# A second Strassen level in the first feed-forward product, with its weight forms streamed from DRAM

## The chip, the core and the metric

The kernel runs on one core of one Trainium2 chip. The metric is the device time of one execution in microseconds, the median of several runs. Work is done by TensorE (matrix products, into the eight PSUM banks of 512 fp32 columns), VectorE, ScalarE and GpSimd (elementwise work), and SyncE, which here only issues DMA transfers. Each engine takes its own instructions in program order and waits for others through semaphores.

## What is computed

Attention over 8 batches, 12 heads, 448 positions and 64 dimensions, with q and k normalized, and then a feed-forward net on the 3584 x 768 result. All in fp32; the two weight matrices come as float64 and are converted by the kernel during unit 0 ("words" in the code).

```python
q_n, k_n = rmsnorm(q, g_q), rmsnorm(k, g_k)
attn = softmax(q_n @ k_n.T / sqrt(64))          # per batch and head
x = (attn @ v).transpose(0, 2, 1, 3).reshape(8 * 448, 12 * 64)
h = np.maximum(x @ w_in, 0.0)                   # w_in 768 x 2048
out = h * h @ w_out                             # w_out 2048 x 768
```

## The kernel before, in words

**Units.** Two batches make a unit (896 rows of x); there are four units, 0 to 3. The feed-forward net of unit u runs while attention makes the x of unit u+1. Attention goes over pairs of heads, 12 pairs per unit; the result of a pair is one tile xT of 128 partitions (two heads' dimensions) by 448 columns (positions), kept transposed. Attention of the first unit runs alone; the last unit's feed-forward net runs alone.

**First level of Strassen.** Both feed-forward products use the Winograd form of Strassen's scheme: seven half-size products P1 to P7 take the place of eight, with sums of the operands ("forms") made before and sums of the products after. For the first product the x of a unit is cut into a 2 x 2 of blocks (by batch, and by the half of the 768 features), and w_in likewise (by halves of features and of hidden columns). `make_x_forms` (L640) and `begin_forms` (L651) turn three chunks each of the x blocks 11, 12, 21, 22 into the seven right-hand operands 11, T1, 21, T2, 22, T3, T4, by two subtractions on VectorE and two on GpSimd (L638). The weight forms 11, 12, S3, 22, S1, S2, S4 are made once, during unit 0, from the 32 pieces of w_in (`convert`, `join_words`, `end_join`, `make_weight_forms`, sums at L974 alternately on VectorE and GpSimd), stored in DRAM as in_forms (L976), and loaded again for units 1 to 3 (`load_in`, L676 to L679). The forms of w_out are handled likewise (`load_out`).

**The feed-forward stream.** `ffn(u)` (L703) is a generator. It goes over four blocks (blk). A block has two calls of `first_products` (L724), each with seven products of three matmuls (128 x 128 weights, 448 columns; L733). The products add up in three PSUM banks, which take three roles in turn. ScalarE copies P1, P5, P6 and P4 out (L740), VectorE adds bank and copy into a tile hid (L753), ScalarE applies relu and square (L754, L755). Four sums of hid per call are made by GpSimd (`hidden_sum`, L769) for the second product. `second_products` (L771) then does the remainder rows (L785) and three times seven products of two matmuls of 384 columns (L814), whose results VectorE adds to the accumulators acc (L855).

**What sets the order.** The order on every engine is written out by hand. The stream yields a cost after each product; `run(until)` (L1018) takes steps of the stream until a cost is reached, and at each step also makes one weight sum, converts weights when they are due (unit 0), and runs one or two waiting tasks of attention (`run_tasks`). The loop over pairs (L1216) runs the stream in even parts of its cost between attention's visits (`visit_among`, `visit_whole`), so that attention's matmuls are spread over the stream. A visit does a pair's scores (L405), exponentials (ScalarE, L413), the products with v (L490, L502) and the denominators (L516, L542); its other work (squares, transposes L339, powers L202, additions L432, DMA issues) is put in the task queues.

**Queues.** All loads and stores of this part go through SyncE in program order: q, k and v (L157, L166, L330, L348, L355), q rows written out and read back in blocks (L314, L330), weights (L679, L684) and results (L860). `load_in` for the tile after the next is issued at the end of P7.

**Room.** In SBUF there are 32 tiles xT (L602), two tiles in_sb (28 forms' chunks each way, 1344 KB), two out_sb, four tiles part (L599), three of words (L596).

The functions the diff touches follow.

## Time and profile before

| what | value |
|---|---|
| median of 3 runs | 1424.97 us (1424.9 to 1426.72) |
| profiled execution, span from first to last instruction | 1427.5 us |
| instructions | 15,477 |
| mean granted TensorE clock | 0.997 |
| busy: TensorE, weight loads, VectorE, ScalarE, GpSimd | 1401.5, 677.4, 660.0, 597.4, 689.3 us |
| DMA | 188.51 MB, mean 132 GB/s |
| first matmul of a first product (L733) | at 137.4 us |
| last matmul of a first product (L733) | at 1388.5 us |

The profiled execution is one more run, with the profiler on; its span stands 2.5 us above the median of the runs. A TensorE instruction of fp32 operands appears as two records, each with its own weight load (PEld). In a timeline a row gives start, duration, engine, line, operation, the tile written and those read, and in brackets the idle time before it and who ended it. In the chain of waits each row is start, duration and the work that the end of the kernel depended on in that stretch.

### The profile page before, as it was taken

The page shows a single profiled execution, that of the slowest core. Times are in us where ns is not written, and L with a number is a line of the kernel's source. Part 1 is how long each engine was busy: PE and PEld are TensorE (multiplying, and loading weights), DVE is VectorE, ACT ScalarE, POOL GpSimd, SP SyncE. Part 2 cuts the span into 40 slices and gives each one's busy share as a digit, 9 for nine tenths or more (in the row PEclk, how much of TensorE's full clock was granted, in tenths as well). Part 3 has the DMA queues.
Part 4 walks back from the last instruction along what each step waited for, and adds up shares of the span by engine and source line. Part 5 has one row for each costly group of instructions (what it writes and reads, how often), then busy time and mean ns, then how long its engine had stood idle before and what let it go on. Part 6 is the DMA issues. An engine that isn't in the chain of part 4 may idle for free.

```text
span 1427.5 us, 15477 instructions
## 1 busy us (share of the span) xinstructions
PE 1401.5 (98%) x4932; PEld 677.4 (47%) x4932; DVE 660.0 (46%) x1233; ACT 597.4 (42%) x1126; POOL 689.3 (48%) x688
## 2 busy tenths in 40 slices
PE   7999999999999999999999999999999999999998
PEld 3333444444444445445454544445444455555554
DVE  5997365886777623324252453224233251132413
ACT  6874466647555254342424334442432303212130
POOL 5666654655556657356455566365462422021111
PEclk9999999999999999999999999999999999999999
DMA  5765336565667573453435454343622242213122
GB/s 139 195 193 151 67 96 196 157 197 164 197 183 218 160 209 94 127 138 99 138 78 172 122 182 126 74 149 87 185 71 89 95 153 79 111 55 127 39 89 80
DMA packets 311007, 188.51 MB, mean 132 GB/s; under 512 B 267524, under 2 KB 295044, under 8 KB 302724
## 3 DMA queue, kind: packets, MB, share of 16 engines
q1 hardware_dynamic: 310624, 187.36, 44.9%
q8 instruction: 41, 0.67, 0.2%
q14 instruction: 50, 0.41, 0.1%
q10 hardware_dynamic: 292, 0.07, 0.0%
HBM read 144.97 MB, written 42.40 MB: 131 GB/s over the span
## 4 chain that ended last, share of the span: by engine, by line
PE 91%; DVE 4%; issue 1%; SPq 1%; POOL 1%; ACT 1%; DMA 1%; DVEq 0%; POOLq 0%; ACTq 0%
PE bank L733 35%; PE bank L814 29%; PE bank L405 9%; PE bank L490 9%; PE bank L785 5%; PE bank L516 1%; PE bank L502 1%; PE bank L533 1%; PE bank L542 1%; SPq L157 1%; DVE acc L855 0%; DVE out_sb L974 0%; PE bank L370 0%; DVE out_sb L952 0%; DMA qk<-in_q_dram 0%
## 5 line engine op out<-in xcount | busy, mean ns | idle before, releaser
L733 PE MATMUL bank<-xT,in_sb 128*128 128x448 f32 x1344 | 515.4, 542 | 0.0
L733 PEld LDWEIGHTS bank<-xT,in_sb 128*128 128x128 f32 x1344 | 252.4, 190 | 260.4 <-issue 250.5
L855 DVE TENSOR_TENSOR acc<-acc,bank 128x384 f32<-128x384 f32 x324 | 173.8, 550 | 232.9 <-PE bank L814 183.7
L814 PE MATMUL bank<-out_sb,hid 128*128 128x384 f32 x768 | 266.6, 487 | 1.6 <-DVE acc L855 1.6
L753 DVE TENSOR_TENSOR hid<-bank,part 128x448 f32<-128x448 f32 x128 | 76.9, 622 | 331.9 <-PE bank L733 331.6
L413 ACT ACTIVATE wT<-bank,rr 128x448 f32<-128x448 f32 x288 | 161.5, 631 | 116.5 <-PE bank L405 85.2
L814 PE MATMUL bank<-out_sb,sums 128*128 128x384 f32 x576 | 204.0, 490 | 3.4 <-DVE acc L855 3.3
L814 PEld LDWEIGHTS bank<-out_sb,hid 128*128 128x128 f32 x768 | 145.4, 190 | 105.6 <-DVE acc L855 3.6
L202 POOL TENSOR_TENSOR rr<-ms,minus_half 128x8 f32<-128x8 f32 (+1 forms) x96 | 146.2, 1523 | 81.1 <-DVE ms L195 69.7
L769 POOL TENSOR_TENSOR sums<-hid 128x384 f32<-128x384 f32 x32 | 32.2, 1007 | 295.7 <-ACT hid L755 295.7
L405 PE MATMUL bank<-qT,kT 64*128 64x448 f32 (+1 forms) x768 | 164.5, 575 | 1.4 <-DVE qT L378 1.1
L754 ACT ACTIVATE hid<-hid 128x448 f32<-128x448 f32 x128 | 73.3, 572 | 197.1 <-DVE hid L753 197.1
L814 PEld LDWEIGHTS bank<-out_sb,sums 128*128 128x128 f32 x576 | 107.7, 190 | 88.2 <-DVE acc L855 8.4
L740 ACT COPY part<-bank 128x448 f32<-128x448 f32 x128 | 67.7, 529 | 170.9 <-PE bank L733 170.9
L432 POOL TENSOR_TENSOR sum<-sum,wT 128x448 f32<-128x448 f32 (+1 forms) x96 | 110.6, 1173 | 10.9 <-ACT wT L413 8.1
L405 PEld LDWEIGHTS bank<-qT,kT 64*128 64x128 f32 (+1 forms) x768 | 55.5, 174 | 104.6 <-issue 76.9
L490 PE MATMUL bank<-wT,vt 128*64 128x448 f32 x480 | 102.8, 549 | 0.0
L785 PE MATMUL bank<-out_sb,hid 128*128 128x384 f32 x256 | 85.6, 488 | 0.0
L432 POOL TENSOR_TENSOR sum<-wT 128x448 f32<-128x448 f32 x48 | 56.7, 1199 | 49.2 <-ACT wT L413 49.2
L554 POOL COPY few<-few 32x14 f32<-32x14 f32 x48 | 9.0, 188 | 144.9 <-DVE few L552 142.9
L192 DVE TENSOR_REDUCE ms<-squares 128x8 f32<-128x512 f32 (+1 forms) x68 | 41.8, 615 | 77.3 <-ACT squares L179 77.3
L755 ACT ACTIVATE hid<-hid 128x448 f32<-128x448 f32 x128 | 73.8, 577 | 4.1
(101 smaller groups left out, 1287.7 us busy)
## 6 DMA issues: line engine op xcount, KB each, us to landing
out_sb<-out_forms SPq DMA_DIRECT2D x24, 1536.0 KB, 9.4
in_sb<-in_forms SPq DMA_DIRECT2D x24, 1344.0 KB, 5.9
words<-in_moe_w_in_dram SPq DMA_DIRECT2D x32, 384.0 KB, 4.0
words<-in_moe_w_out_dram SPq DMA_DIRECT2D x32, 384.0 KB, 3.8
out_forms<-out_sb SPq DMA_DIRECT2D x8, 1536.0 KB, 7.1
in_forms<-in_sb SPq DMA_DIRECT2D x8, 1344.0 KB, 5.9
qk<-in_q_dram SPq DMA_DIRECT2D x96, 96.0 KB, 3.2
qk<-in_k_dram SPq DMA_DIRECT2D x96, 96.0 KB, 2.7
```

The lines of the kernel that those rows point to most:

```text
L202: self.nc.gpsimd.tensor_tensor(out=self.rr[i][:, x, 0 : self.count(i)], in0=ms, in1=self.minus_half.to_broadcast(list(ms.shape)), op=ALU.pow,)
L405: nc.tensor.matmul(sc[some], lhsT=turned[p, 1][r, keys], rhs=turned[p, 0][r, :], start=True, stop=True,)
L413: nc.scalar.activation(new_weights((i, m), e), sc, AF.Exp, scale=rows.rr[i][:, 1, 2 * m + e : 2 * m + e + 1],)
L432: nc.gpsimd.tensor_tensor(out=sums[i, e][some], in0=left[some], in1=weights[key_of(i, m), e][some], op=ALU.add)
L490: nc.tensor.matmul(values_bank(i)[ds(e * D, D), :], lhsT=lasts[i % 2][mine, e, :] if m == NJ else values[i][:, m, e, :], rhs=weights[key_o ...
L733: nc.tensor.matmul(ps, lhsT=w_sb[:, IN.index(left), c, :], rhs=forms[u, c][right], start=first and c == 0, stop=c == NK - 1, skip_group_ch ...
L753: nc.vector.tensor_tensor(out=dst, in0=left, in1=right, op=op)
L754: nc.scalar.activation(dst, dst, AF.Relu)
L755: nc.scalar.activation(dst, dst, AF.Square)
L785: nc.tensor.matmul(ps, lhsT=flat[a][:, t, ds(NT * P, P)], rhs=w_sb[t][:, 2 * a + half, :], start=(a, t) == parts[0], stop=(a, t) == parts[-1],
L814: nc.tensor.matmul(ps, lhsT=lefts[left][:, t, ts(tt, P)], rhs=w_sb[t][:, OUT.index(right), :], start=first and t == 0, stop=t == 1, skip_g ...
L855: nc.vector.tensor_tensor(out=acc, in0=acc, in1=ps, op=ALU.add)
```

## The change

Unit 0 is computed as before. In units 1 to 3 each of the seven first-level products of a block is itself done by a second Strassen level. The two calls of `first_products` of a block are joined: rows of hidden columns of both calls form a 2 x 2 with the first two chunks of the features, the columns are halved (224 positions), and the third chunk is added in plainly. One product then takes 7 + 4 = 11 matmuls of 224 columns in place of 2 x 3 of 448 (12 of 224).

For this:

- **Deep weight forms.** The DRAM copy in_forms is replaced by in_deep: per block seven products with ten 128 x 128 forms each. During unit 0 `deep_steps` stores five slices of the two in_sb tiles of a block as they are (20 stores in all) and makes the others by five sums on four products and five on three, ten per block, on VectorE and GpSimd through the tile more (four buffers), each followed by its own store (40 in all). One step per step of the stream; what is left is done before the block's second product (`make_all_deep`).
- **Streaming.** `load_piece` loads the ten forms of one product (640 KB) into a ring of four places in the two in_sb buffers. The piece four products ahead is asked for when a product has issued its last matmul.
- **Deep x forms.** For each of the seven x forms `deeper` makes three more half tiles and changes one half in place (two subtractions of 224 columns on VectorE, two on GpSimd). They lie in tiles more and words.
- **Room for x.** There are 25 tiles xT in place of 32. Eight of a unit's twelve x tiles that come before the current unit's forms are let go are stored in DRAM (`settle`) and fetched back later (`bring`).
- **A plan of steps.** As the last block of a unit lets go of each form (`let_go`), `follow_plan` makes the next unit's forms, up to two steps per step of the stream.
- **Products and evictions.** `deep_products` interleaves product k with the rest of product k-1, in groups of two or three matmuls. Banks take turns by product; bank 1, which the scores also use, holds one part aside. Partial sums are taken out of a bank while the sum goes on: by ScalarE for P1 and P5, by VectorE otherwise, added to the tiles hid or R (a pair of part tiles). The relu and square of the last half are one VectorE instruction.
- **Hidden sums and remainder rows.** All eight GpSimd sums of a block come at the end of its deep products or at the start of the second product; the remainder-row matmuls are split between the end of the deep products and the first of the second ones.
- **Places of attention's visits.** `place` puts the visits of units 1 and up at chosen costs of the stream (near the end of the deep products, a third into the second products, after the second deep product) in place of even spacing.

In the built program the part that is executed has, beside what the list names, 504 VectorE instructions at the new line L908 (42 per block), 12 copies at L918 and 12 at L1014; 26 of the 40 weight sums stand on VectorE and 14 on GpSimd; there are 84 loads at L798, and 24 stores and 23 loads of x tiles.

```diff
-    in_forms = [dram.tile([P, 7, NK, P], F32, name=f"in_forms{p}") for p in range(NF // 2)]
+    in_deep = [dram.tile([P, 7, 10, P], F32, name=f"in_deep{b}") for b in range(NBLK)]
...
-        return ffn_p.tile([P, S], F32, name="xT", tag="xT", bufs=11 * NK - 1)
+        return ffn_p.tile([P, S], F32, name="xT", tag="xT", bufs=7 * NK + 4)
+
+    def new_more():
+        return ffn_p.tile([P, 3, S // 2], F32, name="more", tag="more", bufs=4)
...
+            def halves(n):
+                c0, c1 = forms[u, 0][name], forms[u, 1][name]
+                h = S // 2
+                b11, b12, b21, b22 = c0[:, 0:h], c0[:, h:S], c1[:, 0:h], c1[:, h:S]
+                t1, t2, t4 = [more[0][:, m] for m in range(3)]
+                engine, dst, left, right = (
+                    (nc.vector, t1, b12, b11), (nc.vector, t2, b22, t1),
+                    (nc.gpsimd, t4, b21, t2), (nc.gpsimd, b12, b22, b12),
+                )[n]
+                less(engine, dst, left, right)()
...
-    def load_in(n):
-        if NF // 2 <= n < B // 2 * NF // 2:
-            in_sb[n] = new_in()
-            nc.sync.dma_start(in_sb[n], in_forms[n % (NF // 2)])
+    def load_piece(n):
+
+        if n >= (B // 2 - 1) * NBLK * 7:
+            return
+        if n % 4 == len(ring):
+            both = ffn_p.tile([P, 2, 10, P], F32, name="in_sb", tag="in_sb")
+            ring.extend((both[:, 0], both[:, 1]))
+        block, k = divmod(n, 7)
+        nc.sync.dma_start(ring[n % 4], in_deep[block % NBLK][:, IN.index(DEEP[k][1])])
...
+    DEEP = [
+        ("P1", "11", "11", "R", None), ("P5", "S1", "T1", "22", None),
+        ("P2", "12", "21", "11", "R"), ("P6", "S2", "T2", "R", "R"),
+        ("P3", "S4", "22", "12", "22"), ("P7", "S3", "T3", "R", "R"),
+        ("P4", "22", "T4", "21", "R"),
+    ]
...
+            if n == 0:
+                multiply(a, lhs(0), rhs["11"], start=True)
+                multiply(b, lhs(3), rhs["T1"])
+                multiply(b, lhs(8), rhs["32"])
...
+                elif base:
+                    add(
+                        both_of(quarter(name, 0), quarter(name, 3)),
+                        both_of(quarter(base, 0), quarter(base, 3)), both_of(a, b),
+                    )
+                else:
+                    nc.scalar.copy(both_of(quarter(name, 0), quarter(name, 3)), both_of(a, b))
+            elif n == 1:
+                multiply(aside, lhs(1), rhs["21"], start=True)
+                multiply(aside, lhs(7), rhs["31"], stop=True)
+                multiply(a, lhs(4), rhs["T2"])
+                put(name, 1, a, base)
+                put(name, 0, aside, name)
+            elif n == 2:
+                multiply(a, lhs(5), rhs["T3"])
+                multiply(b, lhs(6), rhs["22"])
+                multiply(b, lhs(9), rhs["32"], stop=True)
+                put(name, 3, a, name)
+                put(name, 1, b, name)
+            else:
+                multiply(a, lhs(2), rhs["T4"])
+                multiply(a, lhs(8), rhs["31"], stop=True)
+                put(name, 2, a, base)
+                del ab[k], w[k], x[k]
+                load_piece(((u - 1) * NBLK + blk) * 7 + k + 4)
+                if blk == NBLK - 1:
+                    let_go(u, right)
...
+        for k in range(8):
+            if k < 7:
+                step(k, 0)
+            if k:
+                step(k - 1, 2)
+            yield (3 * (k < 7) + 3 * (k > 0)) * COST_DEEP
...
+                step(k, 1)
+            if k:
+                step(k - 1, 3)
...
-        forms_to_store.append(((in_forms if kind == "in" else out_forms)[t], dst))
+        if kind == "out":
+            forms_to_store.append((out_forms[t], dst))
+        elif t % 2:
+            some = deep_steps(t // 2, in_sb[t - 1], dst)
+            sums_to_make.append(lambda: deep_to_make.extend(some))
...
+        def derive(some, n, left, right, op):
+            size = some.stop - some.start
+            made[n] = ffn_p.tile([P, 4, P], F32, name="more", tag="more", bufs=4)[:, 0:size]
+            left, right = [x() for x in (left, right)]
+            next(sum_engines).tensor_tensor(out=made[n], in0=left, in1=right, op=op)
+            nc.sync.dma_start(keep[:, some, n], made[n])
...
+    def place(u, x):
+
+        if u == 0:
+            return COST * x / unit
+        block = LATER // NBLK
+        end = block - COST_SECOND - 2 * COST_DEEP
+        at = [0, end]
+        for b in range(NBLK - 1):
+            at += [b * block + end + block // 3, (b + 1) * block + 84, (b + 1) * block + end]
+        at += [LATER - COST_SECOND // 2, LATER]
+        n, more = divmod(x / VISITS, 1)
+        return at[int(n)] if not more else (at[int(n)] + at[int(n) + 1]) / 2
```

## The prediction

> **What bounds the kernel now.** I read the page first, then the chain of waits in order of time, then the groups, then timelines and the queue's waits.
>
> ```profile
> PE 1401.5 (98%) x4932; PEld 677.4 (47%) x4932; DVE 660.0 (46%) x1233; ACT 597.4 (42%) x1126; POOL 689.3 (48%) x688
> ...
> PE 91%; DVE 4%; issue 1%; SPq 1%; POOL 1%; ACT 1%; DMA 1%; DVEq 0%; POOLq 0%; ACTq 0%
> PE bank L733 35%; PE bank L814 29%; PE bank L405 9%; PE bank L490 9%; PE bank L785 5%; PE bank L516 1%; PE bank L502 1%; PE bank L533 1%; PE bank L542 1%; SPq L157 1%; DVE acc L855 0%; DVE out_sb L974 0%; PE bank L370 0%; DVE out_sb L952 0%; DMA qk<-in_q_dram 0%
> ```
>
> TensorE is the bound: 98% busy and 91% of the chain, and the line that is changed (L733) alone is 35%. No other engine is over half busy. The chain in order of time shows one feed-forward block of the last unit, in which no attention is left:
>
> ```profile
> 1229.84 31.57 PE bank L733 x84
> 1261.40 5.16 PE bank L785 x16
> 1266.57 27.09 PE bank L814 x84
> ```
>
> A first product is 42 matmuls, seen as 84 records: each fp32 matmul is two passes. 31.57 us / 84 = 375.8 ns from pass to pass, with no gap. The groups (busy is the union; the mean of one, 542 ns, [...]overlaps the next):
>
> ```profile
> L733 PE MATMUL bank<-xT,in_sb 128*128 128x448 f32 x1344 | 515.4, 542 | 0.0
> L733 PEld LDWEIGHTS bank<-xT,in_sb 128*128 128x128 f32 x1344 | 252.4, 190 | 260.4 <-issue 250.5
> L855 DVE TENSOR_TENSOR acc<-acc,bank 128x384 f32<-128x384 f32 x324 | 173.8, 550 | 232.9 <-PE bank L814 183.7
> L753 DVE TENSOR_TENSOR hid<-bank,part 128x448 f32<-128x448 f32 x128 | 76.9, 622 | 331.9 <-PE bank L733 331.6
> L740 ACT COPY part<-bank 128x448 f32<-128x448 f32 x128 | 67.7, 529 | 170.9 <-PE bank L733 170.9
> ```
>
> VectorE and ScalarE wait for TensorE in these products, not the reverse. The only short pass in the trace is the transpose, 128 columns over a fresh 128-column weight:
>
> ```profile
> 67.20 0.27 PE L373 MATMUL bank<-wide,qk 128*128 128x128 f32 x1
> 67.31 0.49 PE L370 MATMUL bank<-wide,qk 128*128 128x128 f32 x3
> 67.64 0.27 PE L373 MATMUL bank<-wide,qk 128*128 128x128 f32 x1
> ```
>
> From 67.31 to 67.64 are three passes: 110 ns each.
>
> Where TensorE does stall, VectorE was held by something that has nothing to do with the matmul. In the timeline at a change of unit a subtraction on xT takes 2.62 us (its shortest is 0.607), and 1.63 us of TensorE idle follow:
>
> ```profile
> 827.49 2.62 DVE L638 TENSOR_TENSOR xT<-xT 128x448 f32<-128x448 f32 x1 [0.56 <-POOL xT L610]
> ...
> 830.63 1.56 PE L814 MATMUL bank<-out_sb,hid 128*128 128x384 f32 x4 [1.63 <-DVE acc L855]
> ```
>
> The table by windows gives VectorE's load where it is highest and where it is lowest (after the time: PE, PEld, DVE, ACT, POOL):
>
> ```profile
> 300.00:400.00 100.00, 98.19 (x325) 44.99 (x324) 76.90 (x136) 57.24 (x111) 61.20 (x50) 1.00 0.61 175
> 1286.00:1319.00 33.00, 33.00 (x92) 17.29 (x91) 7.33 (x13) 9.24 (x17) 3.94 (x4) 1.00 0.36 138
> ```
>
> In unit 0, where weights are converted, VectorE is 77% busy and TensorE loses 1.8 us in 100; in the last unit's first product it is 22% busy and TensorE loses nothing. Last, SyncE's waits and the loads:
>
> ```profile
> SPq L679 <- PE bank L733: 245.4, 21, 22.4
> SPq L330 <- DMA q_rows<-qk: 61.5, 32, 4.9
> ...
> out_sb<-out_forms SPq DMA_DIRECT2D x24, 1536.0 KB, 9.4
> in_sb<-in_forms SPq DMA_DIRECT2D x24, 1344.0 KB, 5.9
> words<-in_moe_w_in_dram SPq DMA_DIRECT2D x32, 384.0 KB, 4.0
> ```
>
> SyncE issues in order and stands up to 22.4 us at a weight load. That costs nothing now, because a load is asked for a whole seven-product group ahead.
>
> [...]
>
> **The change, part by part.** Only the first products of units 1 to 3 change, 12 of 16 blocks.
>
> *TensorE passes.* Removed per block: 84 x 375.8 = 31.57 us. Added: 7 products x 11 matmuls x 2 passes = 154 passes of 224 columns, a form the trace doesn't show. Below: half a 448 pass, 187.9 ns. Above: 192 ns, if the next pass had to wait for the end of a 190 ns load that starts 2 ns into the running one; the transposes speak against it (loads of 140 ns, passes every 110). The line through 128 and 448 columns gives 110 + 96 x 0.831 = 189.8[...]. Gain 2.43 us per block, **29.2 us** in 12 (24.0 to 31.6). All of it lies on the chain. The remainder-row and second-product matmuls are the same in number.
>
> *Evictions.* Per block VectorE loses 8 x 0.622 = 5.0 us and gets 8 operations of 448 columns (4 read two strips of a bank) and 36 of 224. For 224 I extend the slope between 384 and 448, (622 - 550)/64 = 1.125 ns: 0.370 us (0.311, half of 448, to 0.550). 8 x 0.622 + 36 x 0.370 = 18.3 us, so +13.3 per block, +160 in all. ScalarE: 8 copies and 16 activations (0.575) become 2 copies of 448, 4 of 224 and 14 activations: 13.4 to 10.5 us. Hidden or not? A product is 22 passes, 4.16 us; it needs about 2.6 us of VectorE. I walked one product: a partial sum must be out of its bank before the next three-matmul group adds to it, and two groups lie between, so every eviction ends about 1.0 us before it is needed. Attention's VectorE work (0.63 us a transpose, up to two tasks per yield) fits into that once or twice in a row, not three times. Cost beyond the cover: a late eviction's lateness plus about 0.1 us for a weight load no longer ahead. I put 0.25 us per block: **+3 us** (0 to 20).
>
> *Hidden sums.* The eight GpSimd sums (1.0 us each) now all stand at the block's end, four of them behind attention's additions (1.17 us). Counting from the sixth product, the last is ready about 1 us before P3 of the second product reads it. **+1 us** (-1 to 8).
>
> *Unit 0.* 40 more sums for the deep weight forms: 26 on VectorE (15 of 512 columns, 11 of 384: about 0.78 and 0.65, 19 us) and 14 on GpSimd (17 us), each with its own store, 20 raw stores beside them instead of 8 large ones (17,920 KB for 10,752). A sum waits for the store four sums earlier (some 4 us, as the 384 KB rows) and some VectorE sums wait for GpSimd ones; behind them in VectorE's queue stand the conversions and evictions. Evictions there have about 4.5 us of cover (two 448-column products), but the stretch is VectorE's fullest. **+4 us** (0 to 15).
>
> *Changes of unit.* 14 more subtractions of 224 columns per unit on VectorE and as many on GpSimd (0.37 and 0.7 us, a little over half of the 448-column ones, 0.61 and 1.14): 5 and 10 us towards a unit's end, and 8 x tiles parked in DRAM and fetched back (224 KB; 192 KB rows land in 2.8 us). The stall shown above (1.63 us) is of this kind. **+1 us** at each of three: +3 (0 to 9).
>
> *Streaming.* 24 loads of 1344 KB become 84 of 640 KB. Between 384 KB (4.0 us) and 1344 KB (5.9) lies 4.5 us (2.8, by size, to 5.9). A load is issued when the product four ahead of its user ends its last matmul; as products are interleaved, two lie between: 8.3 us of cover. It waits for TensorE on SyncE's queue; behind it stand q, k and v loads, needed a visit or more later (some 20 us). Ahead of it may stand a store that waits for GpSimd and block loads that wait for that store (4.9 us at most, plus four issues, 1.9 us in the timeline). 8.3 - 4.5 leaves 3.8 us. **0 us** taken, +1 for single misses (0 to 25).
>
> Sum: -29.2 + 3 + 1 + 4 + 3 + 1 = **-17.2 us**. The profiled execution's span is 1427.5, so 1410.3; the runs' median, 1424.97, is 2.5 below that span, and I take the difference over: **1407.8**.
>
> **Rivals.**
> 1. *All hidden.* Every cover holds: -29.2, 1395.8. For it: 1.0 us of cover everywhere, no stall in the last unit now. Against: VectorE goes from 46% to about 61%, in order, with waits on DMA and GpSimd in its queue.
> 2. *VectorE binds in the deep products.* From 500 to 1100 us the windows have about 35 us of VectorE per 100, some 27 per block of 78 us; a block without attention has 20, so attention adds about 7, half of it in the deep products, to 18.3 us in 29 us of matmuls; if it comes in clumps, 1 us of stall per second product, 28 in these two units, 28/2 = 14 us more: 1422.
> 3. *Pieces come late: slower.* 56 pieces of units 1 and 2 share SyncE's queue with attention. Each late by 0.31 us on average uses up the 17.2 us; at 0.5 us it is 28 us: 1436. For it: waits of 4.9 us ahead of a 3.8 us reserve. Against: these waits are rarely whole when SyncE arrives, and visits lengthen the cover.
> 4. *A 224-column pass isn't half price.* At 205 ns (31.57/154) nothing is gained, and with the other terms 1437. The two loads and passes above speak against it.
>
> **How the numbers follow.** Forecast (1401 to 1415) 0.50; all hidden (below 1401) 0.24; VectorE (1415 to 1428) 0.17, of which 0.05 lie within 0.2%, about what a measurement can tell from no change (1422.1 to 1427.8); late pieces 0.07 and dear passes 0.02, both slower. Faster 0.86, same 0.05, slower 0.09. For 8 in 10: 1395 to 1421 leaves out about 0.05 below and 0.15 above.
>
> **What would show it.** Passes of 189 ns and about 29.2 us of chain for a deep block of the last unit in place of 31.57. Group busy of the new evictions near 0.37 us. TensorE's idle by releaser: VectorE in unit 0 and at unit changes, DMA into in_sb if rival 3 holds. The forecast is wrong if a pass costs over 192 ns, if a deep block of the last unit takes over 30 us, or if in_sb loads appear among TensorE's releasers for more than 5 us.

## The result, and the profile after

The changed kernel takes 1462.07 us (median of 4 runs, 1459.24 to 1466.67) against 1425.85 us (4 runs beside it): a ratio of 1.0254, 95% interval 1.0231 to 1.0277. It is 36 us slower where 17 us faster was forecast. The profiled execution has a span of 1462.1 us (before: 1427.5), so the spans tell of the same 35 us.

The passes did what they should. From the page of the changed kernel, the engines and the group of the new passes (busy us, mean ns of one | idle of the engine just before, and who ended it):

```profile
PE 1395.6 (95%) x5772; PEld 838.7 (57%) x5772; DVE 848.0 (58%) x1727; ACT 563.9 (39%) x1078; POOL 746.4 (51%) x750
...
L921 PE MATMUL bank<-xT,in_sb 128*128 128x224 f32 x1344 | 294.1, 357 | 10.9 <-DMA in_sb<-in_deep 6.1
```

TensorE is less busy in a longer span: 95% of 1462 where it was 98% of 1427. What has grown is its idle time. From start to start two 224-column passes lie 189.0 ns apart (median), as forecast, and one 224-column addition on VectorE, which takes a partial sum out of a bank (an eviction), takes 0.39 us in the timelines, close to the 0.37 forecast.

The chain of waits in order of time, for a block of the last unit, where there is no attention:

```profile
1331.90 27.39 PE bank L921 x144
...
1359.32 0.39 DVE part L908
1359.70 1.38 DVE hid L908 x3
...
1361.92 1.02 PE bank L921 x4
1362.94 1.29 PE bank L1050 x4
```

From 1331.90 to 1362.94 are 31.04 us. In them lie 154 passes (29.1 us) and four passes of the remainder rows that used to come later (1.29 us, like the four of the last line). The rest, about 0.65 us, is TensorE waiting for VectorE's additions near the block's end. From block to block the last three blocks take 62.0 us each instead of 63.8: a gain of 1.8 us, not 2.43.

Where is the rest? I took from the trace, for each stretch between ends of second products, how long it lasted and how TensorE's starts are spaced against what the pass lengths say. (Half clock means a granted clock of 0.5; there the changed kernel's 224-column passes start 373 ns apart instead of 189, at the median. From start to start a stall comes out about 0.16 us longer than in the brackets of a timeline: 2.47 for 2.31 us.)

| stretch | before, us | after, us | idle over 0.2 us, before / after | added by passes at half clock, before / after |
|---|---|---|---|---|
| start and block 0 | 225.0 | 225.2 | 14.1 / 15.6 | 3.1 / 1.6 |
| unit 0, blocks 1 to 3 | 271.9 | 293.7 | 5.4 / 20.8 | 0 / 6.7 |
| unit 1 | 337.3 | 350.5 | 1.8 / 17.4 | 0 / 3.3 |
| unit 2 | 331.3 | 337.1 | 0 / 11.1 | 0 / 1.7 |
| unit 3 | 255.3 | 248.9 | 0 / 2.0 | 0 / 0 |

In sum: passes -28.8, idle +45.6, half clock +10.2, waits under 0.2 us +3.5, and 4.2 that I put down to attention's small matmuls, which overlap each other less (of their 1872 records 1025 start within 60 ns of the one before, and 1061 did before the change): +34.7 us. Who ended most of that idle time is in the table of TensorE's waits (us in total, times, longest):

```profile
PE bank L533 <- ACT wT L413: 15.3, 4, 5.5
PE bank L1095 <- DVE acc L1138: 9.0, 9, 3.3
PE bank L921 <- DVE part L908: 6.1, 4, 2.1
PE bank L921 <- DMA in_sb<-in_deep: 6.1, 3, 3.4
PE bank L921 <- DVE hid L908: 5.6, 9, 1.5
```

The first line is unit 0, the fourth is deep pieces (the ten weight forms of one product) that come late, the others are VectorE; of the second line, 4.9 us in five waits were there before the change too. I follow each to its source.

**Unit 0.** L533 (the softmax denominators) waits for exponentials, and in the timeline these stand behind ScalarE's conversion of weight words. TensorE and ScalarE about 265 us:

```profile
266.48 0.55 ACT L1198 ACTIVATE words<-words 128x384 f32<-128x384 f32 x1 [10.08 <-DMA words<-in_moe_w_out_dram]
```

```profile
271.34 1.76 PE L533 MATMUL bank<-sum,ones 128*64 128x448 f32 x4 [5.49 <-ACT wT L413]
```

ScalarE stands 10.08 us for one piece of words. The words are late because SyncE asked for them late. Its queue in the same timeline (start, time to issue):

```profile
241.41 2.47 SPq L1261 DMA_DIRECT2D in_deep<-in_sb  x3
243.92 2.84 SPq L1263 DMA_DIRECT2D in_deep<-in_sb  x2
...
249.96 0.82 SPq L314 DMA_DIRECT2D q_rows<-qk  x1
...
262.49 0.44 SPq L1184 DMA_DIRECT2D words<-in_moe_w_out_dram  x1
...
263.51 1.11 SPq L1272 DMA_DIRECT2D in_deep<-more  x2
264.72 0.95 SPq L1184 DMA_DIRECT2D words<-in_moe_w_out_dram  x1
```

Before the change the same loads of words stand here:

```profile
257.32 1.00 SPq L901 DMA_DIRECT2D words<-in_moe_w_out_dram  x2
```

Five raw stores of a block take 5.3 us just to issue; each store of a sum takes about 0.55 us more between the loads, so that the 15 stores of a block take SyncE about 11 us. What stands behind the raw stores moves by about as much as they take: the store of q rows is issued at 249.96 (243.72 before), the words at 262.49 and 264.72 (257.32 and 257.95 before). The same happens in blocks 2 and 3, where TensorE stands 4.20 and 5.28 us at L533.

**Late pieces.** At the first block of unit 2 a piece is issued at 890.87, behind loads that had waited for q rows, and TensorE stands for it (at the first block of unit 1 it stands 2.31 us):

```profile
895.53 0.62 PE L921 MATMUL bank<-xT,in_sb 128*128 128x224 f32 x2 [3.37 <-DMA in_sb<-in_deep]
```

**VectorE in order.** In block 7, the last of unit 1 (blocks are counted through all units, from 0; VectorE, timeline):

```profile
801.26 1.43 DVE L650 TENSOR_TENSOR xT<-xT 128x448 f32<-128x448 f32 x1 [0.97 <-DMA xT<-x_rows]
802.61 0.63 DVE L565 STREAM_TRANSPOSE inverse<-few 128x448 f32<-128x448 f32 x1
803.17 0.58 DVE L621 TENSOR_TENSOR xT<-bank,rest 128x448 f32<-128x448 f32 x1
803.68 0.66 DVE L908 TENSOR_TENSOR hid<-hid,bank 128x224 f32<-128x224 f32 x2
```

A form of x that waits for its tile to come back from DRAM, and two of attention's operations, stand ahead of two evictions; TensorE idles 1.50 us for the first, and 2.06 us another 4 us later. In block 5, without a form of x, a transpose (L565) waits 1.43 us for GpSimd, with the same sequel in small (0.63 and 1.00 us). At unit 1's end VectorE waits again:

```profile
864.95 1.53 DVE L650 TENSOR_TENSOR xT<-xT 128x448 f32<-128x448 f32 x1 [2.83 <-POOL xT L622]
```

and TensorE idles 3.26 us for the addition behind it.

### The profile page after: what moved, and what is told of

Its sections match the earlier page's. It is cut to its first block, busy times and chain, and to the rows that moved or that the text cites. A ratio compares the mean times of both kernels' runs of the same rounds, so it can differ in the third digit from the quotient of the medians.

```text
span 1462.1 us, 18011 instructions
## 1 busy us (share of the span) xinstructions
PE 1395.6 (95%) x5772; PEld 838.7 (57%) x5772; DVE 848.0 (58%) x1727; ACT 563.9 (39%) x1078; POOL 746.4 (51%) x750
## 5 line engine op out<-in xcount | busy, mean ns | idle before, releaser
L921 PE MATMUL bank<-xT,in_sb 128*128 128x224 f32 x1344 | 294.1, 357 | 10.9 <-DMA in_sb<-in_deep 6.1
L1095 PE MATMUL bank<-out_sb,hid 128*128 128x384 f32 x768 | 268.8, 487 | 3.8 <-DVE acc L1138 3.8
L921 PEld LDWEIGHTS bank<-xT,in_sb 128*128 128x128 f32 x1344 | 255.3, 192 | 25.0 <-issue 9.0
L870 PE MATMUL bank<-xT,in_sb 128*128 128x448 f32 x336 | 135.4, 557 | 0.0
L908 DVE TENSOR_TENSOR part<-part,bank 128x224 f32<-128x224 f32 (+1 forms) x180 | 69.7, 415 | 97.7 <-PE bank L921 91.9
L432 POOL TENSOR_TENSOR sum<-sum,wT 128x448 f32<-128x448 f32 (+1 forms) x96 | 114.0, 1204 | 0.8
L870 PEld LDWEIGHTS bank<-xT,in_sb 128*128 128x128 f32 x336 | 63.8, 195 | 72.7 <-issue 63.7
L977 ACT ACTIVATE hid<-hid 128x448 f32<-128x448 f32 x84 | 48.4, 576 | 128.5 <-DVE hid L908 128.5
L1050 PE MATMUL bank<-out_sb,hid 128*128 128x384 f32 x256 | 90.3, 491 | 0.0
L908 DVE TENSOR_TENSOR hid<-hid,bank 128x224 f32<-128x224 f32 (+1 forms) x180 | 66.6, 397 | 31.2 <-PE bank L921 28.8
L921 PE MATMUL bank<-more,in_sb 128*128 128x224 f32 x288 | 74.2, 358 | 6.9 <-DVE part L908 6.1
```

The source lines that it names most:

```text
L432: nc.gpsimd.tensor_tensor(out=sums[i, e][some], in0=left[some], in1=weights[key_of(i, m), e][some], op=ALU.add)
L870: nc.tensor.matmul(ps, lhsT=w_sb[:, IN.index(left), c, :], rhs=forms[u, c][right], start=first and c == 0, stop=c == NK - 1, skip_group_ch ...
L908: nc.vector.tensor_tensor(out=dst, in0=left, in1=right, op=ALU.add)
L921: nc.tensor.matmul(ps, lhsT=left, rhs=right, start=start, stop=stop, skip_group_check=True)
L977: nc.scalar.activation(dst, dst, AF.Relu)
L1050: nc.tensor.matmul(ps, lhsT=hid[a].rearrange("p t e s -> p t (e s)")[:, t, ds(NT * P, P)], rhs=w_sb[t][:, 2 * a + half, :], start=(a, t) = ...
```

## The experiments

Eighteen kernels, all edits of the changed kernel. "Above before" is the median less that of the kernel before measured beside it (the changed kernel itself: 36.2 us above). The last three columns are durations of stretches from each run's trace as in the table above (271.9, 668.6 and 255.3 us before; 293.7, 687.6 and 248.9 after). A trace is of one execution, and it contains that execution's half-clock periods; where it lies far from the median, the text says so.

| run | us | above before | ratio to before (95%) | blocks 1-3 | units 1+2 | unit 3 |
|---|---|---|---|---|---|---|
| e1_no_deep_stores | 1444.66 | 17.7 | 1.0123 (1.0099-1.0147) | 275.9 | 685.7 | 249.1 |
| e2_two_raw_stores | 1457.22 | 30.3 | 1.0219 (1.0202-1.0236) | 289.8 | 687.4 | 249.2 |
| e3_four_pieces | 1456.77 | 29.8 | 1.0208 (1.0191-1.0225) | 293.8 | 683.0 | 248.3 |
| e4_even_place | 1480.25 | 53.3 | 1.0368 (1.0345-1.0390) | 293.6 | 707.5 | 248.0 |
| e5_multiply_on_vector | 1457.56 | 29.9 | 1.0216 (1.0194-1.0237) | 293.7 | 683.9 | 248.9 |
| e6_forms_on_vector | 1464.61 | 37.0 | 1.0249 (1.0232-1.0266) | 294.1 | 689.7 | 248.6 |
| e7_stores_gpsimd_queue | 1470.64 | 43.0 | 1.0295 (1.0277-1.0314) | 300.8 | 687.8 | 249.2 |
| e8_pieces_gpsimd_queue | 1474.18 | 46.5 | 1.0323 (1.0306-1.0340) | 294.7 | 699.5 | 248.9 |
| e9_stores_scalar_queue | 1450.51 | 25.0 | 1.0185 (1.0151-1.0219) | 280.9 | 687.3 | 248.6 |
| e10_pieces_scalar_queue | 1460.09 | 34.5 | 1.0236 (1.0219-1.0253) | 293.5 | 687.3 | 248.9 |
| e11_one_task_a_step | 1454.20 | 28.7 | 1.0200 (1.0183-1.0217) | 293.4 | 675.3 | 250.7 |
| e12_all_together | 1433.54 | 8.0 | 1.0058 (1.0037-1.0078) | 278.6 | 670.2 | 252.3 |
| e13_keep_last_forms | 1433.10 | 5.9 | 1.0037 (1.0023-1.0050) | 283.6 | 671.9 | 248.1 |
| e14_split_additions | 1431.20 | 4.0 | 1.0026 (1.0010-1.0042) | 284.5 | 667.0 | 248.0 |
| e15_words_scalar_queue | 1444.39 | 17.2 | 1.0115 (1.0098-1.0133) | 290.6 | 670.3 | 252.3 |
| e16_best | 1438.76 | 11.5 | 1.0081 (1.0067-1.0095) | 289.8 | 667.0 | 248.1 |
| e17_four_words_alone | 1448.03 | 19.9 | 1.0148 (1.0133-1.0164) | 278.0 | 684.1 | 248.7 |
| e18_best_four_words | 1422.13 | -6.0 | 0.9956 (0.9942-0.9969) | 276.8 | 667.0 | 248.0 |

My theory after the trace: three causes in three places (SyncE's queue in unit 0, two late pieces, VectorE's order in units 1 and 2). The rival for unit 0: the 40 additional sums, the only thing that I had priced there.

### Unit 0: the stores, or the sums?

**e1_no_deep_stores.**

```diff
+            if blk == 0:
                 nc.sync.dma_start(keep[:, some, n], made[n])    # and the raw stores likewise
...
-        nc.sync.dma_start(ring[n % 4], in_deep[block % NBLK][...])
+        nc.sync.dma_start(ring[n % 4], in_deep[0][...])
```

> Left out: the 15 stores of deep weight forms of blocks 1 to 3 (the sums that make them stay); units 1 to 3 read block 0's pieces for every block, as many bytes as before. Theory 1 (SyncE's issue of these stores holds up the weight words behind them, ScalarE stands for the words and TensorE for ScalarE in blocks 1 to 3): the waits of ScalarE for words fall back to about 5 and 11 us, the three stalls before the denominators (5.7, 4.4, 5.4 us) and the half-clock periods after them go, unit 0 ends 16 to 22 us earlier, 1440 to 1446 us. Rival (the 40 extra sums on VectorE and GpSimd are what delays unit 0): at most 5 us are won, 1457 or more.

Measured 1444.66 us; blocks 1 to 3 take 275.9 us instead of 293.7, so 17.8 us go with the stores, while all 40 sums are still made. ScalarE's waits for the words of w_out (us in total, times, longest), in the changed kernel and then in e1:

```profile
ACT words L1198 <- DMA words<-in_moe_w_out_dram: 30.1, 5, 10.1
```

```profile
ACT words L1198 <- DMA words<-in_moe_w_out_dram: 8.7, 4, 2.6
```

The sums can have at most the 4.0 us by which these blocks are still longer than before.

**e2_two_raw_stores.**

```diff
-            for n, some in enumerate((upper[:, :, 0], upper[:, :, 1], lower[:, :, 1])):
-                nc.sync.dma_start(keep[:, :, n], some)
-            for n, some in enumerate((upper[:, :, 2], lower[:, :, 2])):
-                nc.sync.dma_start(keep[:, :, 7 + n], some)
+            nc.sync.dma_start(keep[:, :, 0:3], upper)
+            nc.sync.dma_start(keep[:, :, 7:9], lower[:, :, 1:3])
... (forms 2 and 7 change places where they are read)
```

> The five raw stores of a block become two (all three chunks of the upper half, two of the lower), the same bytes in runs of 1536 and 1024 instead of 512; nothing is left out. If SyncE's issue time goes by the number of runs, 5.3 us of issue per block become about 2.1 and the waits behind it shrink by 3: 7 to 12 us faster than the changed kernel, 1450 to 1455. If issue goes by bytes, or if the time lies in the ten stores of sums, no change (1462).

The issue of a block's raw stores shrinks even more than expected, from 5.3 us to 1.2 (0.58 + 0.61 us) for the same bytes. But only 3.9 us come back in blocks 1 to 3 and 6 us in all; the ten stores of sums and their place ahead of the words remain.

**e7_stores_gpsimd_queue** and **e9_stores_scalar_queue** move the stores (with e2's two raw ones) to another engine's queue; e9 issues each one sum later, so that ScalarE finds the sum ready.

```diff
-            nc.sync.dma_start(keep[:, some, n], made[n])
+            nc.gpsimd.dma_start(keep[:, some, n], made[n])     # e7
...
+            stores.append((keep[:, some, n], made[n]))         # e9
+            if len(stores) > 1:
+                nc.scalar.dma_start(*stores.pop(0))
```

> The deep weight forms' stores, the raw ones two per block instead of five, are issued on GpSimd's queue instead of SyncE's; nothing is left out. Theory 1 (SyncE's place in the queue): as good as leaving the stores out, 1440 to 1448. If the issue costs GpSimd as much as it cost SyncE (about 7 us per block) and its sums come late for it: 1448 to 1458.

> The deep weight forms' stores (raw ones two per block) are issued on ScalarE's queue, each one sum later than it is ready; nothing is left out. Theory 1 (SyncE's queue, with the words behind the stores, is the cause in unit 0): SyncE has no store more than before, the stalls at the denominators fall to 1 us or less, 1443 to 1449. Rival (12 issues of about 0.6 us in ScalarE's own order, or its waits for the sums, delay the exponentials just as much): 1455 to 1465.

GpSimd's queue is a miss, worse than the changed kernel: a store costs GpSimd 0.77 us of its own time and, put right behind a sum of VectorE's, waits for it (18.1 us in seven of these waits alone), with attention's additions behind. ScalarE's queue gives 12.8 of the 17.8 us in blocks 1 to 3 back, less than expected: ScalarE still waits 15.8 us for the words of w_out, and stalls of 2.5 and 1.7 us are left at the denominators.

**e17_four_words_alone.** This is the sharpest test: no store is moved; the words are only asked for one piece earlier, and two xT tiles make room for the buffer.

```diff
-        return ffn_p.tile([P, HALF, 2], U32, name="words", tag="words", bufs=3)
+        return ffn_p.tile([P, HALF, 2], U32, name="words", tag="words", bufs=4)
...
-        return ffn_p.tile([P, S], F32, name="xT", tag="xT", bufs=7 * NK + 4)
+        return ffn_p.tile([P, S], F32, name="xT", tag="xT", bufs=7 * NK + 2)
...
-        load_weights(n + 2)
+        load_weights(n + 3)
...
+    load_weights(2)          # at the start, behind 0 and 1
```

> The changed kernel with one edit: a fourth buffer for weight words, so that each piece is asked for three pieces ahead instead of two (about 6 us earlier); for its room two of the 25 xT tiles go. All stores stay on SyncE; nothing is left out. Theory 1 (SyncE reaches the words' loads too late, by up to about 10 us): 6 us of lead take most of unit 0's stalls, 10 to 17 us faster than the changed kernel, 1445 to 1452, less what two xT tiles fewer cost at the changes of unit (0 to 5 us). Rival (ScalarE or SyncE have too much to do in unit 0, whatever the lead): 1458 or more.

1448.03 us, and blocks 1 to 3 in 278.0 us: 15.7 of the 17.8 us, with SyncE's queue as full as it was. (The traced execution took 1443.0 us, 5.0 less than the median; by the medians e17 wins 16.3 us and e1 18.5.) The stores at 239.93 and 242.45 us take 2.48 and 2.83 us as in the changed kernel; ScalarE and TensorE at the place of the 10 us wait in e17's timeline:

```profile
254.80 0.57 ACT L1198 ACTIVATE words<-words 128x384 f32<-128x384 f32 x1
```

```profile
264.41 0.97 PE L533 MATMUL bank<-sum,ones 128*64 128x448 f32 x4
```

Neither line has a wait in brackets; of all of ScalarE's waits for words 2.1 us are left. The stores' traffic is still there too, and a piece of words lands as fast as in the kernel before (4.0 and 3.5 us, before 4.0 and 3.8). So what SyncE has to do is not too much, nor are the transfers slow; the loads were asked for with too little lead for the stores put ahead of them.

**e15_words_scalar_queue** gave the words to ScalarE's queue (on top of e12, below), but one piece ahead instead of two.

```diff
-        load_weights(n + 2)        # SyncE
+        if n:
+            load_weights(n + 1)    # ScalarE, ahead of split_words(n)
```

> As all together, and the weight words too are loaded by ScalarE's queue, one piece ahead instead of two; nothing is left out. If what unit 0 still loses (stalls of 3.1 and 1.5 us at the denominators) is SyncE being late with the words: these fall below 1 us, 3 to 5 us faster than all together, 1428 to 1431. If one piece ahead (about 6 us against about 4 us of landing) is too short: ScalarE stands at each piece, 1436 to 1445.

A miss: blocks 1 to 3 go from 278.6 to 290.6 us. One piece of lead is too short, as its second expectation had it. It left unclear whether words were the cause of what e12 still lost in unit 0; e17 and e18 settled that.

### Late pieces

**e3_four_pieces**

```diff
-        if n >= (B // 2 - 1) * NBLK * 7:
+        if n >= 4:
             return
```

> Left out: every load of a deep weight piece after the first four (the four stay in the ring and are used for all blocks). Theory (pieces are late twice only, at the first block of units 1 and 2, 2.5 and 3.5 us, each with a half-clock period of 3.4 us behind it): about 9 us faster, 1451 to 1455, and no change in units' other blocks. Rival (84 loads waiting on SyncE also hold up attention's q, k, v and row loads, and so the later stalls): 20 us or more, below 1442. Rival 2 (pieces are not what is late): 1460 to 1464.

1456.77 us, 6.4 us closer to the kernel before than the changed one is: below the 9 expected, far from the 20 of the rival. The group of the changed passes that read xT, from 500 to 1200 us, first the changed kernel, then e3:

```profile
L921 PE MATMUL bank<-xT,in_sb 128*128 128x224 f32 x896 | 198.4, 359 | 10.5 <-DMA in_sb<-in_deep 5.7 <-DVE hid L908 4.7
```

```profile
L921 PE MATMUL bank<-xT,in_sb 128*128 128x224 f32 x896 | 196.9, 358 | 4.8 <-DVE hid L908 4.7
```

The 5.7 us for the DMA are gone, VectorE's 4.7 stay. So 80 loads of 640 KB less in the queue bring nothing beyond these two stalls.

**e8_pieces_gpsimd_queue** and **e10_pieces_scalar_queue** issue the same loads on another queue, half a product later.

```diff
-        nc.sync.dma_start(ring[n % 4], ...)
+        nc.gpsimd.dma_start(ring[n % 4], ...)     # e8; nc.scalar in e10
-                load_piece(((u - 1) * NBLK + blk) * 7 + k + 4)
+                pending.append(((u - 1) * NBLK + blk) * 7 + k + 4)   # loaded after step(k, 2) of the next turn
```

> The loads of deep weight pieces are issued on GpSimd's queue, half a product later, instead of SyncE's; nothing is left out. If the two late pieces are late because attention's row stores and loads stand ahead of them on SyncE: both stalls go, as in the run that left the loads out, 1454 to 1458. If GpSimd's waits for TensorE hold up attention's additions behind them: 1462 to 1475.

> The loads of deep weight pieces are issued on ScalarE's queue, half a product later, instead of SyncE's; nothing is left out. If only the two late pieces cost: 1454 to 1458. If ScalarE's waits for TensorE hold up the exponentials and evictions behind them as GpSimd's did: 1462 to 1475.

On GpSimd the load's wait for TensorE takes the whole engine along, and the kernel is 10 us slower than the changed one: the late pieces are gone, but the second stall in each of blocks 5, 7, 9 and 11, where TensorE waits for VectorE, is 3.4 to 3.5 us instead of 1.0 to 2.1. GpSimd's waits in e8:

```profile
POOL in_sb L798 <- PE bank L921: 238.0, 43, 30.0
```

The wait itself isn't new: in the changed kernel SyncE stands 193.2 us for the same reason, and by e3 all of the loads cost no more than the two stalls. On ScalarE the result is neither of the two expected: the DMA no longer ends a stall in these units, but VectorE's share before these passes grows from 4.7 to 7.7 us, and 1.7 us are won in all. In unit 2 the 3.37 us stall went; in unit 1 it moved: VectorE stands 3.68 us in a transpose (L339) that waits for q rows to come back, and TensorE 2.99 us for the evictions behind it.

### VectorE's order in units 1 and 2

**e4_even_place** undoes one part of the change, the chosen places of attention's visits.

```diff
-        if u == 0:
-            return COST * x / unit
+        if True:
+            return (LATER if u else COST) * x / unit
```

> Undone: the new schedule of attention's visits in units 1 to 3; they are spread evenly over the unit's cost, as in the kernel before. Nothing is left out. If the places chosen for visits make the collisions on VectorE (about 11 us in blocks 4 to 6 and 8 to 10 besides the unit changes), they move and shrink: 1452 to 1458. If any place collides with evictions that have 1 us of cover: 1462 to 1475, with more and smaller stalls between deep passes.

17 us slower than the changed kernel, all in units 1 and 2 (707.5 us for 687.6; by the trace 15.4 us more idle time and 9.8 more at half clock, less 5.5 in shorter waits). The second expectation holds in its direction and goes beyond its range, but the stalls are larger, not smaller: 3.6 us in each of blocks 4, 6, 8 and 10, for VectorE. Deep evictions don't bear attention's VectorE work at these places. The chosen places are worth 17 us.

**e5_multiply_on_vector** and **e6_forms_on_vector.**

```diff
-            nc.gpsimd.tensor_tensor(out=xT, in0=xT, in1=inverse[i], op=ALU.mult)
+            nc.vector.tensor_tensor(out=xT, in0=xT, in1=inverse[i], op=ALU.mult)
... (and once more, with inverse.pop(i))
-        less(nc.gpsimd, some["T4"], some["21"], some["T2"])()        # e6 too, and three more such
+        less(nc.vector, some["T4"], some["21"], some["T2"])()
```

> The two multiplications that finish attention's columns (xT by inverse) go from GpSimd to VectorE; nothing is left out. Theory (VectorE stands in its queue for GpSimd, 1.4 us at the second transpose of a pair and 2.8 us at a unit's end, because GpSimd does attention's additions first, and the deep evictions stand behind it): of the stalls 0.8 + 1.2 and 1.7 + 2.2 us in each of units 1 and 2 about 4 go, of the 4.5 us at unit 1's end about 3: 8 to 14 us faster than the changed kernel, 1448 to 1454. Rival (VectorE is short of time, not made to wait: 0.6 us more on it per multiplication makes it worse): 1460 to 1468.

> As the run before, and every subtraction that makes forms of x in units 1 to 3 is on VectorE too (20 more there for each unit, 0.4 to 0.6 us each); nothing is left out. Theory of waits between the two engines: the stalls at units' ends go altogether, 2 to 6 us faster than the run before. Rival (VectorE's time): 9 us more of VectorE in a unit's last deep block, where it is fullest, gives back what was won, 0 to 8 us slower than the run before.

e5 wins 6.3 us by the medians; in its trace units 1 and 2 are 3.7 us shorter, with 5.6 us less idle time and 4.0 us more at half clock. The stalls at unit 1's end go (1.1 and 3.4 us from start to start, with 1.8 us in their place), but of the 0.8 + 1.2 and 1.7 + 2.2 us in unit 1's deep products only 0.4 us go (0.5 + 1.2 and 2.5 + 1.3 remain). There my reading was half right: the wait for GpSimd is gone, and three or four VectorE operations in a row do the same. So the theory of waits between engines falls for the deep products; that it is VectorE's own work in clumps there, the next run tests.

e6, with more work on VectorE, gives back all that e5 had won, as its rival said, but not in the deep products: the stalls there are e5's or less (0.5 + 1.2 us in block 5, one of 2.5 in block 7). It loses in the second products at unit 1's end, where TensorE waits 4.7 us for VectorE instead of 1.0, and by the two pieces, which cost 3.9 and 3.0 us instead of 2.1 each.

**e11_one_task_a_step**, on top of e5, thins the clumps.

```diff
-            follow_plan(2)
-            run_tasks(2 if cost > COST_OUT else 1)
+            follow_plan(1)
+            run_tasks(2 if cost > COST_OUT and first else 1)
```

> As the run with the multiplications on VectorE, and in units 1 to 3 one of attention's tasks and one step of the x forms between two groups of deep passes instead of two; nothing is left out. If the stalls in the deep products (0.5 + 1.2 us in block 5, 2.5 + 1.3 in block 7, the same in the next unit) come from attention's VectorE work in clumps of two or three ahead of evictions with 1 us of cover: they shrink to below 0.6 us each, 4 to 8 us faster than that run, 1449 to 1454. If tasks then pile up at the visits and at units' ends: 1457 to 1466.

Units 1 and 2: 675.3 us (e5: 683.9). The 2.5 + 1.3 us in block 7 are 0.5 + 1.2 now; 1.2 us also stay in block 5 (e14 takes them up). Of the 8.6 us about 5 are idle time and 7 passes at half clock, which e5's execution had more of; shorter waits take some back. By the medians e11 is 3.4 us better than e5, and 1.2 when each is set against the kernel before beside it. Other stalls grew: the late piece at unit 1's start from 2.1 to 4.4 us, and 2.5 us at unit 3's start are new.

### The repairs together

**e12_all_together** is e9, e10 and e11 in one.

> Stores and pieces on ScalarE's queue, multiplications on VectorE, one task a step: the last three runs in one, nothing left out. If the three causes are apart and add: 17 + 5 + 10 us below the changed kernel, 1428 to 1434, about the kernel before. If the freed time is taken by the next releaser (a stall moved, not removed): 1440 to 1455.

8.0 us above before: 28 us better than the changed kernel, more than the three alone (11.2 + 1.7 + 7.5). e11's late piece is gone with e10's edit, and e10's evictions are on time with e11's. Each alone had shown a stall that the other removes.

**e13_keep_last_forms** and **e14_split_additions**, each on top of the one before:

```diff
-        follow_plan(len(plan))                       # in drain
+        follow_plan(len(plan) - 12)                  # the rest one a step in the next unit
...
-                add(to["12"][:, 0], to["12"][:, 0], to["R"][:, 0])            # e14
-                add(quarter("12", 3), quarter("12", 3), quarter("R", 3))
+                some = both_of(quarter("12", 0), quarter("12", 3))
+                add(some, some, both_of(quarter("R", 0), quarter("R", 3)))
```

> As all together, and the last 12 subtractions of x forms (of 22, T3, T4, first read in the fifth product) are not forced out at a unit's end but follow one a step in the next unit; nothing is left out. If the stalls left at the changes of unit (0.5 + 1.3 and 2.5 us behind a run of eight subtractions on VectorE, and a half-clock period) come from that burst: 3 to 6 us faster than all together, 1427 to 1431. If VectorE is short at that place whatever the order (the subtractions are only moved): 1432 to 1436.

> As the run before, and of the additions of R to 12 in the fifth product only what the next eviction overwrites is done ahead of it (one of 448 columns instead of 448 and 224), the rest after it; nothing is left out. Theory (the 1.15 us stall in each unit's second and fourth block and 0.4 us in every block of the last unit is these additions ahead of an eviction with 1 us of cover): each shrinks by 0.4 us or more, 2 to 4 us faster than the run before. If the stall has another cause: no change.

e13's median is inconclusive (5.9 us above before; e12 8.0), and as a time it lies in the range of its rival. Its trace, of an execution 3.1 us above the median, says why: unit 3 is 4.2 us shorter, without the 2.5 us stall and its half clock, so the burst was the cause there. But units 1 and 2 are 1.7 us longer, and in unit 0 the largest stall left was 3.8 us instead of 3.1, and 6.8 us at half clock followed it, which e12 was spared. e14 wins 4.9 us in units 1 and 2 by the traces (the 1.15 us stalls are 0.43 in two blocks and 0.97 in two others), about 2 by the medians; the 0.4 us in each block of the last unit stay, so these have another cause than the expectation gave.

**e16_best** is e14 with e15's edit, and **e18_best_four_words** is e14 with e17's.

> The three last edits on top of all together; nothing is left out. If they are apart and add: 8 to 12 us below all together, 1421 to 1426, at or just under the kernel before. If unit 0's words came no earlier: 1426 to 1430.

> The kernel of the run with split additions (stores and pieces on ScalarE's queue, multiplications on VectorE, one task a step, last forms kept, additions split) with the fourth words buffer and two xT tiles fewer; nothing is left out. If unit 0's last stalls (4.0 and 3.0 us, with 10 us of half clock) are words still late: they go, 7 to 11 us faster than that run, 1420 to 1425, at or under the kernel before. If the missing xT tiles hold up the forms at the changes of unit: 1428 to 1435.

e16 shares e15's fault (blocks 1 to 3: 289.8 us). e18 takes 1422.13 us against 1428.11: 0.44% faster than the kernel before (ratio 0.9942 to 0.9969). It leaves out nothing and beats both kernels. From the page of e18:

```profile
PE 1382.6 (97%) x5772; PEld 834.4 (59%) x5772; DVE 856.0 (60%) x1751; ACT 564.8 (40%) x1078; POOL 724.5 (51%) x726
```

TensorE has the passes of the changed kernel, in a span of 1420.2 us.

## Why the prediction was wrong, step by step

- **TensorE passes, -29.2.** Right: 189.0 ns a pass at the median and 189.5 on average, which makes -28.8 us. The 2.43 us a block were my estimate, between those of the two bounds, 187.9 and 192 ns (2.63 and 2.00); the line through the trace's own passes, 189.8 ns, gives 2.34, or 28.1 us in 12 blocks.
- **Unit 0, +4.** The step that failed most: +22.0, of which 6.7 are passes at half clock. It priced the 40 sums on VectorE and GpSimd and gave each "its own store", but nowhere SyncE's time to issue 15 stores a block, and not what stands behind them on that queue: the weight words, asked for two pieces ahead. The cover (the time between the end of a step and the moment when it is needed) that I had checked, 4.5 us for evictions, was the wrong one; the one that broke was the words' lead. Leaving the stores out gave 17.8 us, lead alone 15.7. With both repairs in e18, blocks 1 to 3 stand 4.9 us above before, about what the step had said for the sums; no run leaves the sums alone out.
- **Streaming, +1.** The mechanism of rival 3 is there, though in two pieces and not in 56: 5.7 us of stalls, 6.4 us by leaving the loads out. The text named the store and the loads that may stand ahead of a piece, and its own figures had a late piece: 4.9 us of waits and 1.9 of issues against a reserve of 3.8 leave 3.0 us, and 2.31 and 3.37 were measured. It was put at 0 because such waits are rarely whole, which held for all but two. The 4.9 us "at most" didn't hold: the longest wait for q rows in the changed kernel is 9.7 us. The sign of being wrong that it had named, in_sb loads among TensorE's releasers for more than 5 us, came true with 6.1.
- **Late evictions, +3.** Mis-sized. The durations were right (0.39 for 0.37 us), the lateness was not: 0.65 us a block even in the last unit, where 0.25 had been taken, and stalls of 0.7 to 2.2 us (from start to start) in four blocks of units 1 and 2, about 12 us. (The 0.1 us that it added to a lateness shows in its own trace: the four passes behind the stall of 1.63 us take 1.56 us, against 1.46 with starts 323 ns apart; that the weight load makes the difference was not separated.) The step itself said that attention's work fits in "once or twice in a row, not three times" and then priced an average; the trace has three in a row at the larger stalls, one of them a subtraction of 1.43 us, and at the smaller ones two behind a wait of 1.43 us. Rival 2 (14 us) had the size of this one, though its second halving, 28/2, has no reason in the text. A deep block of the last unit takes 29.75 us without the remainder rows' passes, just under the 30 that were named as a sign.
- **Changes of unit, +3.** About 9.5 us of stalls where 1.8 had been before, 5.6 of them at the change from unit 1 to 2, in part VectorE's waits for GpSimd (e5). In e12, where those are gone, its own burst of subtractions was behind the stall at unit 3's start (e13).
- **Hidden sums, +1.** No pass in the changed kernel waits for one: 0.
- **Left out altogether: the clock.** 10.2 us more lie in passes at half clock behind the longer stalls, the 6.7 of unit 0 among them.

By units, the forecast was +4 and three times about -7; measured were +22.0, +13.2, +5.8 and -6.4. The sign was lost in the first three. The rivals were taken one at a time, and the range had no case in which two covers fail together; in fact rival 2, the mechanism of rival 3 and the unpriced queue came at once.

**What stays open.** In e18 units 1 and 2 are together only 1.6 us shorter than before, with passes 19.2 us shorter. Its trace has there 9.9 us of stalls over 0.2 us (1.8 before), 1.6 us at half clock, and some 8 us in waits under 0.2 us and in lost overlap. Their last releasers are VectorE's evictions and attention's operations; which order would free them wasn't tried.

## What to carry to other kernels

Price a new transfer by its time in the issuing queue too, list what is queued behind it, and compare the sum with the lead of those loads: here about 11 us of issue a block, on the queue of loads with two pieces of lead, cost 18 us over three blocks, and one more buffer took back 16. When a change leaves 1 us of cover in place of 4.5, count the places where other work stands three in a row on that engine, instead of an average. Ask what else hangs on the queue that waits: here 193.2 us of waits on SyncE cost no more than two stalls (6.4 us by leaving the loads out), while 238.0 us of the same waits on GpSimd, which also computes, made the kernel 10 us slower than the changed one.

## What the runs showed of the hardware that I had not expected

**Behind most stalls of 2 us and more the granted clock was 0.5 for a while.** In the 20 traces of this case each TensorE stall of 3.5 us or more after the first 50 us (47 of them, measured from start to start, the longest 5.9 us) came with a period at granted clock 0.5, of 3.4 or 6.8 us; of those from 2.0 to 3.5 us, 54 of 92 did, and the same 3.43 us stall at unit 1's end went both ways. In the changed kernel's trace the four of 5.65, 4.36, 5.44 and 3.53 us came with periods of 6.8, 3.4, 6.8 and 3.4 us, which began between 3.0 us before the stall's end and 0.9 us after it. Seven periods came behind stalls of only 0.9 to 1.8 us, all seven at attention's products of 64 by 64 (L502), so the length of a stall doesn't decide it alone; what else counts is open. The table by windows for unit 0 (after the time: PE, PEld, DVE, ACT, POOL, then the granted clock), the changed kernel and then e18:

```profile
225.00:495.00 270.00, 251.02 (x799) 113.25 (x798) 194.19 (x336) 140.18 (x273) 164.29 (x137) 0.97 0.71 201
```

```profile
225.00:495.00 270.00, 261.32 (x856) 120.25 (x853) 204.32 (x351) 146.75 (x281) 173.07 (x147) 1.00 0.74 212
```

So by my estimate a stall of 4 us costs up to 5.7 or 7.4 (on top comes half of what of the 3.4 or 6.8 us lies behind the stall; in the changed kernel's unit 0 the three stalls, 15.5 us together, brought 6.7), and a repair that takes it under 3.5 us may win more than its length. It also goes with differences between executions of one kernel: of e14's six, the one with a mean granted clock of 0.998 took 1425.65 us, the others, at 0.993 to 0.995, took 1431.05 to 1433.07.

**The issue of a store isn't free, and doesn't go by bytes.** The same 2,240 KB per block took SyncE 5.3 us in five stores of 512-byte runs and 1.2 us in two stores of 1536- and 1024-byte runs. Whether the number of stores or that of runs makes the time was not separated.
